# Two of six triangular inverses by halves of 16, joined on TensorE, and U's transpose from products of R and T

## The chip, the cores and the metric

The kernel runs on one core of one Trainium2 chip. The metric is the device time of one execution in microseconds (us), given as the median of several runs. The span in a profile, from the first to the last instruction, is some 2 us shorter. The **clock** is the granted clock of the matrix engine (TensorE, PE in the profile) as a share of full speed. In the records it is either 0.50 or 1.00, so a mean of 0.80 over a stretch says that 40% of the stretch ran at half clock.

## The reference, cut to what matters

```python
# r, k, v, w, a, b: (4 batches, 8 heads, 768 tokens, 40)
for t in range(S):
    y[:, :, t] = einsum('bhd,bhde->bhe', rt, state)
    Sa = einsum('bhde,bhe->bhd', state, at)
    state = state * wt[:, :, None, :] - einsum('bhd,bhe->bhde', Sa, bt)
    state = state + einsum('bhd,bhe->bhde', vt, kt)
# then, on all 3072 tokens (320 features, 2048 hidden)
h = x @ w_in
out = (h * clip(h + 3, 0, 6) / 6) @ w_out
```

## The kernel before

The scan over tokens is done in blocks of 64 tokens. Two batches make a unit of work, so there are 24 units ("steps"), and four units make a group. Within a block the effect of tokens on each other is a triangular system for each head. Its inverse T is worked out once for each group, for 32 heads and both batch halves together. There are six groups, so six inverses. The 64x64 inverse is put together from two inverses of 32x32 (substitution on VectorE, one row after another) and one off-diagonal block, which TensorE makes by two products (`third_block`).

```python
def invert(F, third):
    fb = inv.tile([P, L, L], F32, name="fb")
    nc.vector.transpose(out=..., in_=F[:, :, 0:L]...)
    x = inv.tile([P, L, L], F32, name="x", tag="x", bufs=1)
    # ... GpSimd masks fb into x, ones on the diagonal
    for i in range(1, L - 1):                  # 30 rows, two instructions each
        nc.vector.tensor_tensor(out=pv, in0=..., in1=..., op=ALU.mult)
        yield
        nc.vector.tensor_tensor(out=rest, in0=rest, in1=pv, op=ALU.add)
        yield
    # ... tb and tt: the inverse transposed, as TensorE wants it
def third_block(F, tb, tt, n):                 # products of F and tb, evicted as zs, then of tt and zs
    ...
```

A step takes T and makes U from it, then U's transpose, which feeds the scores:

```python
nc.tensor.matmul(out=up[x][half(x ^ s), pr, :], lhsT=tinv[...], rhs=R[...])   # U
...
x = turn_pairs(U)                              # four 128x128 transposes
UT = turned("UT"); nc.scalar.activation(out=UT[:], in_=x[:], func=AF.Copy)
x = scores(UT, RT, swap=True)
```

Each `yield` gives the builder of the program a place to put something else. In the first inverse this is the conversion of the feed-forward weights (`weights`), in the second it is feed-forward products (`pieces`). The program order of each engine is fixed at build time.

```python
while side:            # first group's inverse
    aside(1, 1)        # one step of the inverse, one step of conversion
...
for _ in range(16):    # second group's inverse
    aside(2)
    pieces(0.75)       # feed-forward products
...
# a feed-forward job may start only when:
i in ready and converted[0] >= (PIECES // 2 if i < SPLIT and r == 0 else PIECES)
```

A request for a feed-forward product is dropped when its job is not yet available. So the speed of the conversion decides how much feed-forward work lies early in the program.

Of the kernel before, what the change touches and what calls it, by code (L numbers as in the profile page):

```python
# [8 lines left out]
F32 = mybir.dt.float32  # L9
I32 = mybir.dt.int32  # L10
U32 = mybir.dt.uint32
ALU = mybir.AluOpType
# [4 lines left out]
P = 128  # L17
BL = 64
HB = BL // 2
L = 32  # L20
SLOT = 64


# [6 lines left out]
def kernel(  # L30
# [105 lines left out]
    def padded(t, name):  # L136
        nc.gpsimd.memset(t[:, :, D:SLOT], PADS.get(name, 0.0))
        return t
# [33 lines left out]

    values = [padded(const.tile([P, H, SLOT], F32, name=f"V{i}"), "V") for i in range(AHEAD)]
    inputs["R"] = padded(const.tile([P, H, SLOT], F32, name="R"), "R")

    tinv = const.tile([P, NH, BL], F32, name="tinv")

# [322 lines left out]
        yield DONE  # L500


    def invert(F, third):



        fb = inv.tile([P, L, L], F32, name="fb")
        nc.vector.transpose(out=fb[:].rearrange("p t s -> p s t"),
                            in_=F[:, :, 0:L].rearrange("p h s -> p s h"))
        x = inv.tile([P, L, L], F32, name="x", tag="x", bufs=1)  # L510
        nc.gpsimd.affine_select(out=x[:], in_=fb[:], pattern=[[1, L], [-1, L]],  # L511
                                compare_op=ALU.is_gt, fill=0.0, base=0, channel_multiplier=0)
        nc.gpsimd.memset(_ap(x[:], 0, [[L + 1, L]]), 1.0)
        for _ in range(3):
            yield
        for i in range(1, L - 1):
            n = L - 1 - i
            prod = inv.tile([P, L * L // 4], F32, name="prod")
            pv = prod[:, 0:n * i].rearrange("p (r j) -> p r j", j=i)
            nc.vector.tensor_tensor(  # L520
                out=pv, in0=_ap(x[:], (i + 1) * L + i, [[L, n], [0, i]]),
                in1=_ap(x[:], i * L, [[0, n], [1, i]]), op=ALU.mult,
            )
            yield
            rest = x[:, i + 1:L, 0:i]
            nc.vector.tensor_tensor(out=rest, in0=rest, in1=pv, op=ALU.add)  # L526
            yield
        tb = inv.tile([P, NH, L], F32, name="tb", tag="fb")
        nc.vector.transpose(out=tb[:].rearrange("p h t -> p t h"), in_=x[:])  # L529
        yield  # L530

        tt = inv.tile([P, NH, L], F32, name="tt")
        nc.vector.transpose(out=tt[:].rearrange("p h j -> p j h"),
                            in_=x[:].rearrange("p r j -> p j r"))
        third.append((F, tb, tt))
        for z in range(0, P, BL):
            yield
            nc.scalar.activation(out=tinv[z:z + L, :, 0:L], in_=tb[z:z + L], func=AF.Copy)
            nc.gpsimd.tensor_copy(tinv[z + L:z + BL, :, L:BL], tb[z + L:z + BL])
        yield  # L540

    def third_block(F, tb, tt, n):
        heads = slice(n * H, (n + 2) * H)
# [27 lines left out]
    def step(i):  # L571
# [21 lines left out]
                                     lhsT=o["at"][half(s, D), pr, half(q)],  # L593
                                     rhs=st[half(s, D), q, pr, 0:D], start=True, stop=True)
        yield PE
        R = tmp.tile([P, 2, NPR, D], F32, name="R")
        for s in range(2):
            nc.vector.tensor_tensor(out=R[:, s], in0=rp[s][:], in1=o["EV"][:, s], op=ALU.add)
        yield DONE
# [39 lines left out]
        yield DONE  # L639


        ysp = [ps_any([P, 2, 2, BL]) for _ in range(2)]
        for j in range(2):
            for q in range(2):
# [26 lines left out]
        for q in range(2):  # L671
            nc.vector.tensor_tensor(out=st[:, q, :, 0:D], in0=sn[q][:], in1=st[:, q, :, 0:D],  # L672
                                    op=ALU.add)
        yield DONE

        x = turn_pairs(U)
        yield PE
        UT = turned("UT")
        nc.scalar.activation(out=UT[:], in_=x[:], func=AF.Copy)
        yield DONE  # L680

        x = scores(UT, RT, swap=True)
# [177 lines left out]
    def by_twos(first, steps, mixed, rate, fill={}):  # L860


        chains = [prepared(first + i) for i in range(NU)]
        for t in range(TWOS):

            order = [0, 1] if t < STAGES else []
            order += [2, 3] if t > 5 else []
            if t == 3:
                order = [2, 3, 0, 1]
            for i in order:  # L870
                run(chains[i], steps if t > 10 else 0, fill.get(t, 0), mixed)
                pieces(rate / 2)
            if t == 10:
                side.append(invert(group_F[-1], third))
            yield


# [29 lines left out]
    for t in range(LAST + OWN):  # L907
        for i in range(NU):
            if 0 <= t - APART * i < OWN and t - APART * i != 11:
                if t - APART * i < 2:  # L910
                    block(i, t - APART * i)
                run(chains[i], weight=3)
        if t == LAST + 2:
            seconds()
            for name in "WA":
                fetch(name, NU + 1)
            third.clear()
            second_group = by_twos(NU, 3, 0, 1.25)
        if t in (LAST + 6, LAST + 8):

            name = "BK"[t > LAST + 6]
            others[name] = second(name)
            fetch(name, NU + 1)
        if t >= LAST + 6:
            next(second_group)
        elif t >= OWN + 1:
            pieces(1)
# [26 lines left out]
    def slot(i, rates, begin):  # L954
# [2 lines left out]
        before, own_chain[0] = own_chain[0], own  # L957
        for j, stages in enumerate((
                (before, own, ahead), (before, own, ahead, block, own), (block, own, ahead),
                (own, own, ahead), (own, pieces, ahead), (own, own, ahead), (own, ahead),  # L960
                (own, ahead))):
            if j == begin:
                side.append(invert(group_F[-1], third))
# [64 lines left out]
```

## Time and profile before

| | before |
|---|---|
| time, median of 3 runs | 882.01 us (881.49 to 888.24) |
| TensorE busy | 786.8 us, 89% of the span |
| VectorE busy | 536.8 us, 61% |
| mean granted clock | 0.94 |
| fifth state product (first of the second group) starts | 224.3 us |

### The profile page before, as it was taken

Reading aid. Unit: us, or ns where it says so; the run is one execution under the profiler, and the core shown is the slowest. Engines: PE = TensorE matmul, PEld = TensorE weight load, DVE = VectorE, ACT = ScalarE, POOL = GpSimd, SP = SyncE. Lnnn points to the kernel's source line nnn. Section 1 sums busy time; section 2 is a strip of 40 time slices with the busy share of each in tenths; the row PEclk is TensorE's granted clock in tenths of the full one; section 3 lists DMA queues with packets and bytes.
Section 4 is the critical chain, followed back from the end, with each engine's and each line's share of the span. In section 5 each row is a group of like instructions: output and inputs, shape, how many; then the busy total and the mean of one; then the engine's idle time right before and its main releaser. Section 6 shows DMA issues by size and latency. Waiting matters only on the chain.

```text
span 880.6 us, 34839 instructions
## 1 busy us (share of the span) xinstructions
PE 786.8 (89%) x15456; PEld 665.2 (76%) x15456; DVE 536.8 (61%) x1141; ACT 291.2 (33%) x670; POOL 148.8 (17%) x318
## 2 busy tenths in 40 slices
PE   4711977798799999999999999999999998999998
PEld 4511865686688888788888888888888887888886
DVE  7999678968854597643697454696455746222211
ACT  1334644232334322433323433233443223222211
POOL 4321011221121220321121122112012201000000
PEclk9755579998899999999999999999999999999999
DMA  6543344431223221222220222231232101000000
GB/s 132 93 103 102 103 112 97 75 64 24 39 41 64 54 46 30 56 38 47 55 56 17 52 48 48 41 57 33 41 57 45 25 15 26 18 20 19 18 17 16
DMA packets 175974, 45.00 MB, mean 51 GB/s; under 512 B 157904, under 2 KB 173264, under 8 KB 175824
## 3 DMA queue, kind: packets, MB, share of 16 engines
q1 hardware_dynamic: 174768, 42.61, 24.3%
q8 instruction: 122, 2.00, 0.9%
q10 hardware_dynamic: 1056, 0.16, 0.1%
q14 instruction: 28, 0.23, 0.1%
HBM read 34.08 MB, written 3.93 MB: 43 GB/s over the span
## 4 chain that ended last, share of the span: by engine, by line
PE 72%; DVE 5%; POOL 2%; issue 1%; ACT 0%; DMA 0%; SPq 0%; POOLq 0%; DVEq 0%; ACTq 0%
PE o L787 21%; PE h L763 18%; PE any L337 7%; PE h L768 6%; PE any L355 3%; PE any L665 2%; PE any L694 2%; PE any L429 2%; PE any L549 1%; PE any L647 1%; PE any L626 1%; PE any L561 1%; PE any L592 1%; PE any L611 1%; PE any L492 1%
## 5 line engine op out<-in xcount | busy, mean ns | idle before, releaser
L787 PE MATMUL o<-wout,gt 128*128 128x320 f32 x768 | 231.2, 442 | 0.5 <-DVE gt L774 0.5
L763 PE MATMUL h<-xt,win 128*128 128x128 f32 x1536 | 194.6, 278 | 0.0
L763 PEld LDWEIGHTS h<-xt,win 128*128 128x128 f32 x1536 | 184.2, 193 | 6.1
L787 PEld LDWEIGHTS o<-wout,gt 128*128 128x128 f32 x768 | 138.4, 191 | 50.5 <-issue 1.0
L774 DVE SCALAR_TENSOR_TENSOR gt<-gt,h 128x512 f32<-128x512 f32 x96 | 61.5, 682 | 83.1 <-ACT gt L773 82.9
L773 ACT ACTIVATE gt<-h,three 128x512 f32<-128x512 f32 x96 | 60.7, 683 | 116.1 <-PE h L768 116.0
L364 DVE COPY_PREDICATED score<-mask,any 128x256 f32<-128x256 int32 x143 | 54.9, 438 | 68.0 <-PE any L355 67.7
L520 DVE TENSOR_TENSOR prod<-x 128x30 f32<-128x30 f32 (+9 forms) x180 | 66.2, 368 | 10.0 <-POOL x L511 6.5
L526 DVE TENSOR_TENSOR x<-x,prod 128x30 f32<-128x30 f32 (+9 forms) x180 | 63.0, 350 | 4.8
L704 POOL TENSOR_TENSOR yg<-ys,gam 128x512 f32<-128x512 f32 x24 | 31.1, 1295 | 186.9 <-DVE ys L701 147.5
L768 PE MATMUL h<-xt,win 64*128 64x128 f32 x768 | 56.7, 288 | 0.0
L768 PEld LDWEIGHTS h<-xt,win 64*128 64x128 f32 x768 | 47.4, 190 | 6.1 <-issue 2.2
L549 PE MATMUL any<-tb,F 32*32 32x32 f32 x768 | 17.5, 203 | 34.8 <-DVE tb L529 34.0
L578 ACT ACTIVATE RT<-any 128x512 f32<-128x512 f32 x24 | 14.3, 596 | 91.5 <-PE any L337 91.5
L451 POOL MEMSET Kt<- 128x24 f32 x24 | 2.8, 118 | 238.0 <-PE any L694 238.0
L549 PEld LDWEIGHTS any<-tb,F 32*32 32x32 f32 x768 | 15.8, 118 | 36.0 <-issue 35.2
L379 DVE TENSOR_TENSOR_SCAN prods<-wm,start 128x528 f32<-128x528 f32 x24 | 30.4, 1267 | 19.2 <-ACT wm L376 17.4
L672 DVE TENSOR_TENSOR state<-any,state 128x160 f32<-128x160 f32 x48 | 13.1, 315 | 47.0 <-PE any L665 47.0
L404 DVE RECIPROCAL rgam<-prods 128x256 f32<-128x256 f32 x24 | 41.5, 1729 | 0.0
L390 DVE RECIPROCAL gam<-prods 128x256 f32<-128x256 f32 x24 | 41.3, 1734 | 0.0
L498 ACT ACTIVATE EV<-any 64x160 f32<-64x160 f32 x92 | 24.8, 294 | 43.6 <-PE any L492 43.1
L246 ACT ACTIVATE parts<-parts,low 128x256 uint32<-128x256 uint32 x40 | 20.3, 508 | 55.6 <-DVE parts L244 55.4
(138 smaller groups left out, 1193.6 us busy)
## 6 DMA issues: line engine op xcount, KB each, us to landing
raw<-in_moe_w_out_dram SPq DMA_DIRECT2D x20, 256.0 KB
B<-in_b_dram SPq DMA_DIRECT2D x48, 80.0 KB
K<-in_k_dram SPq DMA_DIRECT2D x48, 80.0 KB
V<-in_v_dram SPq DMA_DIRECT2D x96, 40.0 KB
R<-in_r_dram SPq DMA_DIRECT2D x96, 40.0 KB
out_dram<-ob SPq DMA_DIRECT2D x48, 80.0 KB
W<-in_w_dram SPq DMA_DIRECT2D x40, 80.0 KB
A<-in_a_dram SPq DMA_DIRECT2D x40, 80.0 KB
```

The source lines that it names most:

```text
L337: nc.tensor.transpose(out=o[:, n, :], in_=x[:, 2 * n:2 * n + 2, :].rearrange("p s e -> p (s e)"), identity=ident[:])
L364: nc.vector.copy_predicated(out=x[:, 4 * i:4 * i + 4, :], mask=mask4, data=o[i][:])
L390: nc.vector.reciprocal(gv[:, :, 0:HB], prods[:, :, 0, 1:HB + 1][:, :, ::-1])
L404: nc.vector.reciprocal(rv[:, :, HB:BL], prods[:, :, 1, 1:HB + 1])
L520: nc.vector.tensor_tensor(out=pv, in0=_ap(x[:], (i + 1) * L + i, [[L, n], [0, i]]), in1=_ap(x[:], i * L, [[0, n], [1, i]]), op=ALU.mult,)
L526: nc.vector.tensor_tensor(out=rest, in0=rest, in1=pv, op=ALU.add)
L549: nc.tensor.matmul(out=zp[x][z:z + L, h, :], lhsT=F[z + L:z + BL, n * H + h, L:BL], rhs=tb[z + L:z + BL, n * H + h, :], start=True, stop=True,
L763: nc.tensor.matmul(out=hp[c][:, i, :], lhsT=win[:, t, j * P:(j + 1) * P], rhs=xt[:, t, :], start=(t == 0 and i == 0), stop=False)
L768: nc.tensor.matmul(out=hp[c][:, i, :], lhsT=win2[half(c), (j0 + i) * P:(j0 + i + 1) * P], rhs=xt[half(c), 2, :], start=False, stop=(i == N ...
L773: nc.scalar.activation(out=gt[:], in_=hp[c][:], func=AF.Relu, bias=three[:], scale=1.0)
L774: nc.vector.scalar_tensor_tensor(out=gt[:], in0=gt[:], scalar=6.0, in1=hp[c][:], op0=ALU.min, op1=ALU.mult)
L787: nc.tensor.matmul(out=op[:], lhsT=gts[c][:, n, :], rhs=wout[:, c * HJ + r * NQ + n, :], start=((split or r == 0) and c == 0 and n == 0), ...
```

## The change

The intent: the first two inverses hold up TensorE, so they are made shorter on VectorE by solving two blocks of 16 at once (28 instructions in place of 60), and TensorE joins the halves. UT no longer waits for U: it comes straight from R and T. Left out of the cut below: R gets one fixed tile of its own (`RR`), and one fetch for the second group comes a step later.

```diff
-    def invert(F, third):
+    def invert(F, third, by_halves=False):
...
+        size, count = (L2, 2) if by_halves else (L, 1)
+        blocks = [size * (L + 1), count]
-        for i in range(1, L - 1):
+        for i in range(1, size - 1):
...
+        if by_halves:
+            yield from join_halves(F, tb, tt)
+    def join_halves(F, tb, tt):
+        for h in range(NH):                    # z: 128 products of 16 columns
+            for i in range(P // L):
+                nc.tensor.matmul(out=zp[i][z:z + L2, h, :], lhsT=F[z:z + L, h, 0:L2],
+                                 rhs=tb[z:z + L, h, L2:L], ...)
+        # six yields, zh = z (ScalarE), six yields
+        for h in range(NH):                    # x: 128 products of 16 columns
+            for i in range(P // L):
+                nc.tensor.matmul(out=xp[i][z:z + L2, h, :], lhsT=tt[z:z + L2, h, 0:L2],
+                                 rhs=zh[z:z + L2, h, L2:L], ...)
+        # tinv = x (ScalarE); lower part: 2 products on the identity, 64 products; four yields; tt
...
+        up = [ps_any([P, 2, P]) for _ in range(2)]      # U's transpose: 32 products
+        nc.tensor.matmul(out=up[x][half(rs), j, half(x ^ s)],
+                         lhsT=RR[half(x), s, pr * D:pr * D + SLOT],
+                         rhs=tinv[half(x), n * H + 4 * s + pr, :], ...)
-        x = turn_pairs(U)
-        UT = turned("UT")
...
-                side.append(invert(group_F[-1], third))
+                side.append(invert(group_F[-1], third, by_halves=True))   # groups 1 and 2 only
...
-                (own, own, ahead), (own, pieces, ahead), (own, own, ahead), (own, ahead),
+                (own, own, ahead), (own, own, pieces, ahead), (own, own, ahead), (ahead,),
```

More of the change, by code (lines that the diff above doesn't have):

```diff
@@ L20 @@
 L = 32
+L2 = L // 2
 SLOT = 64
@@ L174 @@
     inputs["R"] = padded(const.tile([P, H, SLOT], F32, name="R"), "R")
+    RR = const.tile([P, 2, NPR * D + SLOT - D], F32, name="RR")
+    nc.gpsimd.memset(RR[:, :, NPR * D:], 0.0)
     tinv = const.tile([P, NH, BL], F32, name="tinv")
@@ L513, in invert @@
         nc.gpsimd.memset(_ap(x[:], 0, [[L + 1, L]]), 1.0)
+        if by_halves:
+            nc.gpsimd.memset(x[:, L2:L, 0:L2], 0.0)
         for _ in range(3):
             yield
-        for i in range(1, L - 1):
-            n = L - 1 - i
+        size, count = (L2, 2) if by_halves else (L, 1)
+        blocks = [size * (L + 1), count]
+        for i in range(1, size - 1):
+            n = size - 1 - i
             prod = inv.tile([P, L * L // 4], F32, name="prod")
-            pv = prod[:, 0:n * i].rearrange("p (r j) -> p r j", j=i)
+            pv = _ap(prod[:], 0, [[n * i, count], [i, n], [1, i]])
             nc.vector.tensor_tensor(
-                out=pv, in0=_ap(x[:], (i + 1) * L + i, [[L, n], [0, i]]),
-                in1=_ap(x[:], i * L, [[0, n], [1, i]]), op=ALU.mult,
+                out=pv, in0=_ap(x[:], (i + 1) * L + i, [blocks, [L, n], [0, i]]),
+                in1=_ap(x[:], i * L, [blocks, [0, n], [1, i]]), op=ALU.mult,
             )
             yield
-            rest = x[:, i + 1:L, 0:i]
+            rest = _ap(x[:], (i + 1) * L, [blocks, [L, n], [1, i]])
             nc.vector.tensor_tensor(out=rest, in0=rest, in1=pv, op=ALU.add)
@@ L534, in invert @@
                             in_=x[:].rearrange("p r j -> p j r"))
-        third.append((F, tb, tt))
+        third.append((F, tinv[:, :, L:BL] if by_halves else tb, tt))
         for z in range(0, P, BL):
-            yield
+            if not by_halves:
+                yield
             nc.scalar.activation(out=tinv[z:z + L, :, 0:L], in_=tb[z:z + L], func=AF.Copy)
             nc.gpsimd.tensor_copy(tinv[z + L:z + BL, :, L:BL], tb[z + L:z + BL])
+        if by_halves:
+            yield from join_halves(F, tb, tt)
@@ L540, in invert @@
         yield
+    def join_halves(F, tb, tt):
+        zh = inv.tile([P, NH, L], F32, name="zh", tag="x", bufs=1)
+        nc.gpsimd.memset(zh[:, :, 0:L2], 0.0)
+        zp = [ps_any([P, NH, L2]) for _ in range(P // L)]
+        for h in range(NH):
+            for i in range(P // L):
+                z = i * L
+                nc.tensor.matmul(out=zp[i][z:z + L2, h, :], lhsT=F[z:z + L, h, 0:L2],
+                                 rhs=tb[z:z + L, h, L2:L], start=True, stop=True,
+                                 tile_position=(z, z))
+        for _ in range(6):
+            yield
+        for i in range(P // L):
+            z = i * L
+            nc.scalar.activation(out=zh[z:z + L2, :, L2:L], in_=zp[i][z:z + L2], func=AF.Copy)
+        for _ in range(6):
+            yield
+        xp = [ps_any([P, NH, L2]) for _ in range(P // L)]
+        for h in range(NH):
+            for i in range(P // L):
+                z = i * L
+                nc.tensor.matmul(out=xp[i][z:z + L2, h, :], lhsT=tt[z:z + L2, h, 0:L2],
+                                 rhs=zh[z:z + L2, h, L2:L], start=True, stop=True,
+                                 tile_position=(z, z))
+        yield
+        for i in range(P // L):
+            z = i * L
+            x = i % 2 * L + L2
+            nc.scalar.activation(out=tinv[z:z + L2, :, x:x + L2], in_=xp[i][z:z + L2],
+                                 func=AF.Copy)
+        lp = [ps_any([P, NH, L2]) for _ in range(2)]
+        for i in range(2):
+            z = i * BL
+            nc.tensor.matmul(out=lp[i][z:z + L], lhsT=ident[z:z + L, z:z + L],
+                             rhs=tt[z:z + L, :, 0:L2], start=True, stop=False,
+                             tile_position=(z, z))
+        for h in range(NH):
+            for i in range(2):
+                z = i * BL
+                nc.tensor.matmul(out=lp[i][z:z + L, h, :], lhsT=zh[z:z + L2, h, :],
+                                 rhs=tt[z:z + L2, h, 0:L2], start=False, stop=(h == NH - 1),
+                                 tile_position=(z, z))
+        for _ in range(4):
+            yield
+        for i in range(2):
+            z = i * BL
+            nc.scalar.activation(out=tt[z:z + L, :, 0:L2], in_=lp[i][z:z + L], func=AF.Copy)
@@ L595, in step @@
         yield PE
-        R = tmp.tile([P, 2, NPR, D], F32, name="R")
+        R = RR[:, :, 0:NPR * D].rearrange("p s (r d) -> p s r d", d=D)
         for s in range(2):
@@ L639, in step @@
         yield DONE
+        up = [ps_any([P, 2, P]) for _ in range(2)]
+        for j in range(2):
+            for s in range(2):
+                for x in range(2):
+                    for rs in range(2):
+                        pr = 2 * j + rs
+                        nc.tensor.matmul(out=up[x][half(rs), j, half(x ^ s)],
+                                         lhsT=RR[half(x), s, pr * D:pr * D + SLOT],
+                                         rhs=tinv[half(x), n * H + 4 * s + pr, :],
+                                         start=True, stop=True)
+        yield PE
+        UT = turned("UT")
+        for x in range(2):
+            nc.scalar.activation(out=UT[:, 2 * x:2 * x + 2], in_=up[x][:], func=AF.Copy, scale=-1.0)
+        yield DONE
         ysp = [ps_any([P, 2, 2, BL]) for _ in range(2)]
@@ L673, in step @@
                                     op=ALU.add)
-        yield DONE
-        x = turn_pairs(U)
-        yield PE
-        UT = turned("UT")
-        nc.scalar.activation(out=UT[:], in_=x[:], func=AF.Copy)
         yield DONE
@@ L918 @@
             second_group = by_twos(NU, 3, 0, 1.25)
-        if t in (LAST + 6, LAST + 8):
-            name = "BK"[t > LAST + 6]
+        if t in (LAST + 7, LAST + 8):
+            name = "BK"[t > LAST + 7]
             others[name] = second(name)
```

## The prediction

> **What bounds the kernel now.** I read the windows view first, cut at the events that the change touches (columns: busy time of each engine with its number of instructions, granted clock, DMA share, GB/s).

> ```profile
> 44.50:55.50 11.00, 2.73 (x64) 2.49 (x64) 10.61 (x35) 3.15 (x9) 5.34 (x9) 0.50 0.53 128
> 55.50:81.70 26.20, 0.00 (x0) 0.00 (x0) 26.20 (x92) 9.71 (x26) 0.00 (x0) 0.50 0.31 90
> 81.70:126.00 44.30, 35.60 (x851) 31.54 (x852) 33.21 (x101) 26.38 (x58) 5.79 (x12) 0.54 0.37 99
> 126.00:154.50 28.50, 22.31 (x555) 17.67 (x554) 22.72 (x65) 13.95 (x36) 4.79 (x8) 1.00 0.45 114
> 154.50:193.60 39.10, 33.98 (x739) 29.58 (x732) 31.26 (x39) 10.70 (x30) 8.45 (x22) 1.00 0.42 71
> 193.60:234.50 40.90, 30.95 (x385) 26.25 (x383) 36.14 (x77) 11.04 (x24) 8.44 (x19) 0.84 0.20 35
> 234.50:868.00 633.50, 626.76 (x12327) 529.75 (x12327) 339.23 (x679) 202.37 (x452) 99.76 (x201) 1.00 0.20 38
> ```

> From 234.5 us on TensorE is busy 626.8 of 633.5 us: there only TensorE work counts, and whatever the front leaves undone is paid in full at the end. From 55.5 to 81.7 TensorE does nothing and VectorE is never idle: this is the first group's inverse, alternating with the conversion of the weights. The second inverse lies in 193.6 to 234.5, where TensorE is idle 10 us. The timeline shows what ends these waits (start, duration, in brackets the idle time before and its releaser):

> ```profile
> 79.70 1.90 DVE L529 STREAM_TRANSPOSE tb<-x 128x1024 f32<-128x1024 f32 x1
> ...
> 81.74 1.92 PE L549 MATMUL any<-tb,F 32*32 32x32 f32 x64 [26.26 <-DVE tb L529]
> ...
> 87.74 1.92 PE L561 MATMUL any<-zs,tt 32*32 32x32 f32 x64
> ...
> 122.74 1.13 PE L355 MATMUL any<-RT,UT 40*64 40x64 f32 x32 [2.65 <-ACT UT L679]
> ...
> 229.88 1.92 PE L549 MATMUL any<-tb,F 32*32 32x32 f32 x64 [4.95 <-DVE tb L529]
> ```

> The two groups of instructions that the change cuts, from the page's table of groups (busy us, mean ns, idle before):

> ```profile
> L520 DVE TENSOR_TENSOR prod<-x 128x30 f32<-128x30 f32 (+9 forms) x180 | 66.2, 368 | 10.0 <-POOL x L511 6.5
> L526 DVE TENSOR_TENSOR x<-x,prod 128x30 f32<-128x30 f32 (+9 forms) x180 | 63.0, 350 | 4.8
> ```

> 180 of each are 30 for each of six inverses, so one inverse costs (66.2 + 63.0)/6 = 21.5 us of VectorE.

> [...] clock 0.50 from 44.5 to 81.7. [...] the timeline has TensorE back to back from 86.6 to 111.9 us on small products, still at 0.50, and full clock holds only from about 126, when the first 128x128 feed-forward products come. So I don't count on the join's tiny products to warm the clock. [...] 64 instructions of 40x32 tiles (L429 at 22.00 us, full clock) end after 0.85 us; less the last one's own 0.22 us that is 9.8 ns each. [...] the 128x30 update at 44.95 us took 0.87 us under a GpSimd product and 0.18 us at 79.27 us without.

> **The change, part by part.**

> *Substitution.* Two blocks of 16 in one instruction: 28 instructions in place of 60, of 28 to 112 elements. In the late part of the first inverse, five such instructions of 58 to 108 elements and five conversion steps took 78.63 - 76.42 = 2.21 us, 0.44 us a pair. 28 pairs are 12.4 us. Add four masked copies (1.5 us) and some 1.5 us of blocking by GpSimd at the beginning: from 44.6 to about 59.5 us, then the 1.9 us transpose, so TensorE starts at 61.5 rather than 81.7.

> *Join.* 128 products of 16 columns for z, 128 for x, 2 identity products of 512 columns and 64 of 32 columns; each is two instructions here (768 for the 384 feed-forward contractions). At about 11 ns (above, with four row positions), z and x take 256 x 11 = 2.8 us each. The last 128 instructions have two positions like L549, whose 64 take (1.92 - 0.2)/63 = 27 ns each at half clock: 3.4 us; identity some 1.7 us at half clock. Evictions are 586 ns each (the row of L555, 32x512): four for z and four for x, 2.4 us each, two for the lower part. One after the other: z to 64.5, eviction to 67.0, x to 70.0, then lower part to 75.1, third-block products to 76.9, their eviction to 78.2, with two or three ScalarE conversion steps between. L561 starts at 78.3 in place of 87.74: **-9.4 us**. The inverse gains 20 us, of which the join eats 11.

> *U's transpose.* Four 128x128 transposes (0.44 us back to back) give way to 32 instructions of 64x64 tiles, for which 64 take 1.09 us in L694, so 0.55 us. Over some 20 steps at the bound, 20 x 0.07 (taking half of the difference as hidden by pipelining) is **+1.4 us**. Two evictions of about 0.38 replace one of 0.6; ScalarE is not the bound. TensorE waited 4.7 us in all for UT, nearly all before 145 us (0.92, 2.65 and 1.12). UT is now ready two stages earlier. But the longest of these stood behind a ScalarE conversion step which waited for a weight transfer, so I count half: **-2.5 us**.

> *What moves: conversion and feed-forward.* The first inverse carried one conversion step with each of its own. With some 17 steps fewer it leaves conversion behind: by the order of instructions 14 pieces stood before the first state scaling, now 10. Four pieces at about 1.85 us (five VectorE steps) go into the second group's preparation. All 40 must be converted before the second feed-forward job may start, and requests made before that are lost. Counting in program order before the fifth step's first state product: before 92, 40 and 32 products of the three feed-forward lines, after 64, 32 and 22. At 0.112, 0.068 and 0.27 us an instruction (L763 x16 in 1.79, L768 x16 in 1.09, L787 x8 in 2.16), two each, the difference is 6.3 + 1.1 + 5.4 = **12.7 us** of TensorE work, which stays nearly 12 to 14 us at every later step. It is paid after 234.5, where TensorE has no slack. Taking it out of 154.5 to 193.6 gives little back: VectorE is busy 31.3 of 39.1 there, loses two pairs of feed-forward evictions and a sum (about 1.8 us net) and gains 5.6 us of conversion. I set that stretch unchanged.

> *Second inverse.* Without conversion between, dependent instructions of about 100 elements come every 0.29 us (203 to 205 us). 28 are 7.6; with blocking, masked copies and feed-forward evictions and GpSimd's mask before them, tb is ready some 20 us after the begin of its first transpose instead of 36. From there TensorE is bound: z 2.8, 16 feed-forward products 3.6, x 2.8, lower part 2.8 at full clock, then 9.2 of feed-forward, step products and transposes before L561's counterpart: 41.6 us in all against 234.48 - 193.63 = 40.9. **+0.7 us**: the idle time goes, and join work of the same size takes its place.

> Sum: 882.0 - 9.4 - 2.5 + 0.7 + 12.7 + 1.4 = 884.9.

> **Rivals.** *The join is issue-bound at half clock.* If its 16-column products take 27 ns as L549 does, z and x take 7 us each, the first group gains only 1 us and the time is about 893. For it: all 64-column products of 81.7 to 112 have 27 ns. Against: four row positions and narrow weights, and 9.8 ns seen at full clock. *The deferred feed-forward work is not lost.* If the preparation stretch shrinks by half of what leaves TensorE, because TensorE is continuous from 171.5 to 201 there, the time is about 878. *The clock returns earlier.* The new order puts U's products, scores and UT's products, all full-array tiles, one after another; before, such a stretch at 108 to 112 did release the clock for 4 us. Full clock from 100 on would save part of the 26 us of half-clock products, perhaps 6 us, VectorE allowing: about 878. *A whole 20 us gain arrives* (the join hidden, nothing deferred): 862; speaks against it that no other TensorE work stands in program order beside the first join, and that the lag of feed-forward work is in the order itself.

> **Range and chances.** The second and third rival are each likelier than the first, so I put the point under the sum: 880. Each main term has an error of 4 to 6 us, together about 10: range 867 to 893. 2% is 17.6 us. To be faster by that, the deferred work would have to be free as well; to be slower, both joins would have to cost double. Chances 0.11, 0.84 and 0.05.

> **What would show it.** In the changed kernel: the first tb transpose at about 59 us; L561's counterpart at 76 to 80 us; clock still 0.50 in the join; z and x products near 11 ns apart; the second group's preparation as long as before with less feed-forward work in it; TensorE continuous from the second join on; and at the end a longer unbroken run of feed-forward work, by 12 us, than before after the last step. Wrong if the first join lasts over 25 us, if conversion waits for transfers more than before, or if the preparation stretch shrinks by 8 us or more.

## More of the kernel before

From the page of the kernel before: busy time of TensorE and its number of products, the granted clock in 40 equal slices of the span (tenths), and one of the transfer queues (packets, MB, share):

```profile
PE 786.8 (89%) x15456; PEld 665.2 (76%) x15456; DVE 536.8 (61%) x1141; ACT 291.2 (33%) x670; POOL 148.8 (17%) x318
...
PEclk9755579998899999999999999999999999999999
...
q8 instruction: 122, 2.00, 0.9%
```

TensorE is almost always busy after the first quarter. The clock is half from slice 3 to 5.

## The result, and the profile after

The changed kernel took **917.19 us** (median of 4 runs, 915.26 to 919.73). Before took 881.75 us beside it (4 runs). The ratio is 1.0389, with a 95% interval of 1.0331 to 1.0446. So it is slower by 3.9%, where 880 was predicted with a range up to 893.

The parts of the page that answer those above:

```profile
PE 825.5 (90%) x17416; PEld 698.0 (76%) x17416; DVE 516.0 (56%) x1077; ACT 302.7 (33%) x714; POOL 149.5 (16%) x323
...
PEclk8755668597899999999999999999999998999999
...
q8 instruction: 137, 2.24, 1.0%
```

TensorE has 1,960 more products and is busy 39 us longer. There are 15 more packets in the instruction queue.

VectorE's saving is real. Groups of instructions of the stretch of the first two inverses (30 to 300 us), first before, then after (busy us, mean ns):

```profile
L526 DVE TENSOR_TENSOR x<-x,prod 128x30 f32<-128x30 f32 (+14 forms) x60 | 21.5, 358 | 1.0
L520 DVE TENSOR_TENSOR prod<-x 128x30 f32<-128x30 f32 (+14 forms) x60 | 21.4, 357 | 3.5 <-POOL x L511 2.6
```

```profile
L535 DVE TENSOR_TENSOR x<-x,prod 128x28 f32<-128x28 f32 (+6 forms) x28 | 9.0, 323 | 0.5
L529 DVE TENSOR_TENSOR prod<-x 128x28 f32<-128x28 f32 (+6 forms) x28 | 7.9, 283 | 1.8 <-POOL x L516 1.4
```

42.9 us of substitution have become 16.9 us. The windows of the changed kernel, cut at the same events as the prediction's windows (62.4 is the first join product, 85.2 the counterpart of L561, 196.2 the begin of the second inverse, 248.4 its L561 counterpart):

```profile
44.50:62.40 17.90, 2.76 (x65) 2.56 (x65) 17.90 (x62) 7.07 (x20) 4.24 (x10) 0.54 0.52 133
62.40:85.20 22.80, 13.53 (x712) 11.14 (x712) 10.07 (x27) 11.96 (x22) 4.00 (x8) 0.50 0.23 58
85.20:126.00 40.80, 34.70 (x873) 30.46 (x872) 26.16 (x84) 22.36 (x54) 2.75 (x5) 0.58 0.38 103
126.00:154.50 28.50, 23.54 (x521) 18.62 (x522) 23.85 (x70) 13.63 (x35) 3.97 (x7) 0.85 0.45 122
154.50:196.20 41.70, 32.08 (x706) 26.57 (x705) 35.14 (x55) 13.74 (x40) 9.09 (x23) 0.75 0.40 73
196.20:248.40 52.20, 42.80 (x1016) 35.88 (x1015) 23.76 (x47) 15.48 (x30) 9.34 (x21) 0.80 0.13 25
248.40:900.00 651.60, 639.53 (x12951) 542.91 (x12951) 340.41 (x681) 204.14 (x474) 98.70 (x201) 0.99 0.19 38
```

Two things stand out. In the first join (second line) TensorE is busy only 13.5 of 22.8 us, though VectorE is busy less than half of that time. The stretch of the second inverse (sixth line) takes 52.2 us where it took 40.9. The waits of TensorE around the first inverse and join say what the idle time is (line, releaser, us in total, times, longest). Before, 55 to 90 us:

```profile
PE any L549 <- DVE tb L529: 26.3, 1, 26.3
```

After, 62.0 to 85.3 us:

```profile
PE any L563 <- DVE parts L253: 7.4, 1, 7.4
PE any L563 <- issue: 4.9, 2, 2.8
PE any L577 <- issue: 3.5, 2, 2.6
PE any L577 <- ACT zh L570: 0.9, 2, 0.5
```

The wait of 26.3 us is down to 7.4 us, as intended. (The view names L253, which ended last, at 62.38 us; the transpose of tb ended at 62.25.) But 8.4 us are new, in four gaps whose releaser is "issue". That is time in which the engine waited for nothing that the profile shows, so for no semaphore of another engine.

The second join in the timeline of the changed kernel (start, duration, idle before it and its releaser):

```profile
217.37 2.16 PE L563 MATMUL any<-tb,F 32*16 32x16 f32 x175 [1.92 <-DVE tb L538]
221.11 0.86 PE L563 MATMUL any<-tb,F 32*16 32x16 f32 x81 [1.58 <-issue]
221.91 6.21 PE L836 MATMUL h<-xt,win 128*128 128x128 f32 x32
228.04 1.34 PE L577 MATMUL any<-zh,tt 16*16 16x16 f32 x143
230.13 1.06 PE L577 MATMUL any<-zh,tt 16*16 16x16 f32 x111 [0.75 <-issue]
...
233.86 3.28 PE L595 MATMUL any<-tt,zh 16*32 16x16 f32 x117 [0.73 <-issue]
```

The gaps are here too, 3.1 us in all. The 32 feed-forward products between z and x take 6.2 us. The same 32 at full clock took 3.73 us in the kernel before, at 210.12 us of its timeline.

**Where the time went.** I followed the start of each step's state product through both traces. The table gives its shift against the kernel before (us). The last column is what is added after the 24th product.

| stretch | shift of after against before | added in this stretch |
|---|---|---|
| up to the 4th product (first inverse) | -0.8 | -0.8 |
| 4th to 6th (second preparation and inverse) | +11.4 | +12.2 |
| 6th to 24th product | +22.2 | +10.8 |
| after the 24th product (feed-forward tail) | +34.4 | +12.2 |

So four things have to be explained: a gain of 9 us that didn't come, 12 us at the second inverse, a slow creep of 11 us, and a tail of 12 us. Only the tail was in the prediction.

### The profile page after: what moved, and what is told of

Same layout as the page of the kernel before. It is cut to its first block, busy times and chain, and to the rows that moved or that the text cites. A ratio compares the mean times of both kernels' runs of the same rounds, so it can differ in the third digit from the quotient of the medians.

```text
span 915.0 us, 38729 instructions
## 1 busy us (share of the span) xinstructions
PE 825.5 (90%) x17416; PEld 698.0 (76%) x17416; DVE 516.0 (56%) x1077; ACT 302.7 (33%) x714; POOL 149.5 (16%) x323
## 4 chain that ended last, share of the span: by engine, by line
PE 72%; DVE 4%; issue 2%; POOL 1%; ACT 1%; DMA 0%; SPq 0%; DVEq 0%
PE o L860 20%; PE h L836 19%; PE any L341 5%; PE h L841 5%; PE any L359 3%; PE any L767 2%; PE any L744 2%; PE any L433 2%; PE any L611 1%; PE any L710 1%; PE any L688 1%; PE any L623 1%; PE any L654 1%; PE any L673 1%; DVE tb L538 1%
## 5 line engine op out<-in xcount | busy, mean ns | idle before, releaser
L860 PE MATMUL o<-wout,gt 128*128 128x320 f32 x768 | 234.3, 447 | 0.2 <-DVE gt L847 0.2
L836 PE MATMUL h<-xt,win 128*128 128x128 f32 x1536 | 200.2, 285 | 0.5 <-DVE gt L847 0.5
L836 PEld LDWEIGHTS h<-xt,win 128*128 128x128 f32 x1536 | 189.9, 199 | 6.5 <-DVE gt L847 0.7
L860 PEld LDWEIGHTS o<-wout,gt 128*128 128x128 f32 x768 | 140.3, 194 | 51.9 <-issue 3.0
L847 DVE SCALAR_TENSOR_TENSOR gt<-gt,h 128x512 f32<-128x512 f32 x96 | 61.7, 685 | 134.6 <-ACT gt L846 134.5
L535 DVE TENSOR_TENSOR x<-x,prod 128x84 f32<-128x84 f32 (+14 forms) x148 | 55.3, 374 | 3.1
L529 DVE TENSOR_TENSOR prod<-x 128x84 f32<-128x84 f32 (+14 forms) x148 | 48.5, 328 | 9.3 <-POOL x L516 5.3
L383 DVE TENSOR_TENSOR_SCAN prods<-wm,start 128x528 f32<-128x528 f32 x24 | 30.5, 1271 | 17.5 <-ACT wm L380 16.6
L774 DVE TENSOR_TENSOR ys<-any,ys 128x256 f32<-128x256 f32 x48 | 18.1, 418 | 30.2 <-PE any L767 30.2
L878 ACT ACTIVATE ob<-o 128x320 f32<-128x320 f32 x23 | 10.1, 437 | 64.7 <-issue 37.8
```

Source lines behind the costliest of these rows:

```text
L529: nc.vector.tensor_tensor(out=pv, in0=_ap(x[:], (i + 1) * L + i, [blocks, [L, n], [0, i]]), in1=_ap(x[:], i * L, [blocks, [0, n], [1, i]]) ...
L836: nc.tensor.matmul(out=hp[c][:, i, :], lhsT=win[:, t, j * P:(j + 1) * P], rhs=xt[:, t, :], start=(t == 0 and i == 0), stop=False)
L847: nc.vector.scalar_tensor_tensor(out=gt[:], in0=gt[:], scalar=6.0, in1=hp[c][:], op0=ALU.min, op1=ALU.mult)
L860: nc.tensor.matmul(out=op[:], lhsT=gts[c][:, n, :], rhs=wout[:, c * HJ + r * NQ + n, :], start=((split or r == 0) and c == 0 and n == 0), ...
```

## The experiments

The outputs are right. The steps are compared with those of the kernel before in the same way as above.

### Taking the change apart

`inverse_only` has both inverses by halves, but U's transpose, its places in the schedule and the transfers as before:

```diff
-        up = [ps_any([P, 2, P]) for _ in range(2)]      # the 32 products for UT
+        x = turn_pairs(U)                                # four transposes, at the old place
```

> The inverse by halves in both groups, U transposed as before. Theory A (the inverse does nearly all the harm: join held by gaps in the supply of instructions, feed-forward work deferred, clock lost): 25 to 34 us over the kernel before, and the profile keeps a creep of some 8 us between the sixth and the last step. Rival B (U's products, 28 more instructions a step, cause the 10.8 us that the changed kernel loses between the sixth and the last step): 20 to 24 us over before, without that creep.

`ut_only` keeps the old inverses and has the new UT:

```diff
-                side.append(invert(group_F[-1], third, by_halves=True))
+                side.append(invert(group_F[-1], third))
```

> U's transpose by products, both inverses in the old way. Theory A: within 4 us of before, possibly 1 to 3 us faster because the early waits for UT go. Rival B: 8 to 11 us slower than before, lost evenly over the steps.

`first_only` and `second_only` have the new UT, and halves in one of the two groups:

```diff
+        t0 = first                             # the group's first unit
-                side.append(invert(group_F[-1], third, by_halves=True))
+                side.append(invert(group_F[-1], third, by_halves=(t0 == 0)))   # first_only
+                side.append(invert(group_F[-1], third, by_halves=(t0 > 0)))    # second_only
```

> As the changed kernel, but only the first group's inverse by halves. Theory A: the deferred feed-forward work (12.7 us) is all from the first group, since only there does the conversion of weights ride on the inverse; with the loss of clock in the second group's preparation 12 to 18 us over before. Rival C (the joins are the loss and both cost the same): about half of the changed kernel's 35 us, and so no difference between this one and the next.

> As the changed kernel, but only the second group's inverse by halves. Theory A: no feed-forward work is deferred; the join stands in the way of TensorE for some 20 us where the old inverse left it idle for 10: 8 to 15 us over before. Rival C: 17 us, the same as the first group alone.

Measured (3 rounds; before 883.84 us, 7 runs; the shifts are of one profiled execution each):

| kernel | median, us | ratio (95%) | 4th product | 4th to 6th | 6th to 24th | tail |
|---|---|---|---|---|---|---|
| inverse_only | 908.70 | 1.0257 (1.0197 to 1.0317) | -1.0 | +13.9 | +1.9 | +12.3 |
| ut_only | 885.79 | 1.0007 (0.9958 to 1.0056) | +1.8 | +1.8 | +2.8 | -0.3 |
| first_only | 908.33 | 1.0262 (1.0208 to 1.0315) | -0.3 | +4.6 | +8.3 | +12.2 |
| second_only | 898.34 | 1.0130 (1.0072 to 1.0188) | -0.7 | +13.6 | +2.5 | -0.3 |

What follows: the UT products alone cost nothing that can be told from zero. The tail of 12.2 us comes with halves in the *first* group, whatever else is there. Of the 12 to 14 us between the 4th and 6th product, most come with halves in the *second* group; without them it is 1.8 or 4.6. The first group by halves gains at most 1 us by the fourth product, which is no more than single profiles differ there: `second_only`, with the old first inverse, has -0.7, and `ut_only` +1.8. The creep is large only where halves in the first group and the new UT come together.

### Is it the number of instructions?

In the trace of the changed kernel the first join's products come in runs of 125 to 128 between the gaps, at some 10 ns a product (128 in 1.24 us). The transfer records show packets of 16,384 bytes on the instruction queue, six of them in the join. The page has 17,416 pairs of a load and a product for 137 packets, and 15,456 for 122 before: 127 pairs a packet in both. So by my estimate from these counts a packet brings the instructions of about 128 pairs. The four gaps of the first join end 2.3 to 2.5 us after the begin of such a packet.

```diff
+    dummy = ps_any([P, NH, 16])
+    for h in range(320):                      # ready long before, never read
+        z = h % 4 * L
+        nc.tensor.matmul(out=dummy[z:z + 16, h // 4 % NH, :], lhsT=ident[z:z + L, 0:16],
+                         rhs=ident[z:z + L, 16:32], ...)
     while side:
         aside(1, 1)
```

> The kernel before, with 320 products of 32x16 on the identity (640 pairs of load and product, nothing to wait for, never read) put where TensorE idles during the first inverse. Theory (instruction supply): bursts of about 128 pairs at some 10 ns a pair with standing gaps of 2 to 3 us between them that no semaphore explains, in all 16 to 19 us. Rival (the gaps in the join come from its own waits): one unbroken run of about 6.5 us. The kernel's time should hardly move, as TensorE idles there for 26 us.

Measured: one run, 884.18 us. Its timeline on TensorE, from the first of these products to the first of the kernel's own:

```profile
55.72 1.24 PE L890 MATMUL any<-ident 32*16 32x16 f32 x126
58.34 1.26 PE L890 MATMUL any<-ident 32*16 32x16 f32 x128 [1.38 <-issue]
62.34 1.26 PE L890 MATMUL any<-ident 32*16 32x16 f32 x128 [2.74 <-issue]
66.62 1.26 PE L890 MATMUL any<-ident 32*16 32x16 f32 x128 [3.02 <-issue]
70.35 1.26 PE L890 MATMUL any<-ident 32*16 32x16 f32 x128 [2.46 <-issue]
73.81 0.23 PE L890 MATMUL any<-ident 32*16 32x16 f32 x2 [2.19 <-issue]
82.06 1.92 PE L549 MATMUL any<-tb,F 32*32 32x32 f32 x64 [8.03 <-DVE tb L529]
```

This is the mechanism by itself. The 640 pairs took 18.3 us, in runs of exactly 128 with gaps of 1.4 to 3.0 us and not one semaphore. The transfer records of the same trace have five instruction packets, starting at 55.76, 59.72, 64.15, 67.72 and 71.46 us. The next run of products starts 2.58, 2.62, 2.47, 2.63 and 2.35 us after each. Four runs of 128 take (73.81 - 58.34)/4 = 3.87 us each, which is **30 ns a pair**, against 9.8 ns within a run. The rival's 6.5 us is excluded.

Do other transfers hold the packets up? They took 0.32 of the transfer engines' time in these 18.3 us and 0.05 in the second join of the changed kernel (217.3 to 237.1 us), and there too the gaps end 2.4 to 2.6 us after the begin of a packet. So the delay from a packet was no longer at 0.32 than at 0.05. And "issue" alone is not the sign: the wait of 2.4 us that the kernel before has in its second preparation ends 5.3 us after the last such packet, and what it is stays open.

`join_bf16` then takes instructions out of the join. The z and x products work on the upper halves of their words, so each is one pair and not two (with both mendings the stretch from the second inverse to the fifth state product has 667 products in the trace, against 920 in `catch_up`), with everything else the same. It is less exact on purpose.

```diff
-                nc.tensor.matmul(out=zp[i][...], lhsT=F[z:z + L, h, 0:L2],
-                                 rhs=tb[z:z + L, h, L2:L], ...)
+                nc.tensor.matmul(out=zp[i][...], lhsT=F[z:z + L, h, 0:L2].bitcast(BF16)[:, 1::2],
+                                 rhs=tb[z:z + L, h, L2:L].bitcast(BF16)[:, 1::2], ...)
```

> The changed kernel with the 128 z and 128 x products of each join on the upper halves of their words, so that each is one load and one product in place of two: 256 pairs fewer in each join, everything else the same; the result is allowed to be less exact, on purpose. Theory (the join is limited by the supply of instructions, some 128 pairs per 3.7 us): the number of standing gaps in a join falls by two, so each join is 4 to 8 us shorter and the time 8 to 14 us below the changed kernel's, 903 to 909. Rival (the gaps come from something else than the number of instructions, for instance the waits for the banks or the half clock): same gaps, under 4 us gained.

Measured (3 rounds): 902.46 us (898.86 to 907.35), ratio 1.0219 (1.0167 to 1.0270). That is 14.7 us below the changed kernel's median, a little over the range that I had given. The waits in its first join, 62 to 80 us:

```profile
PE any L564 <- DVE tb L539: 7.3, 1, 7.3
PE h L578 <- DVE win L269: 3.7, 1, 3.7
PE any L578 <- ACT zh L571: 1.3, 3, 0.4
```

There is no "issue" gap left. What now shows is a wait of 3.7 us ahead of x, while ScalarE copies to tinv, converts and then evicts z (the first eviction starts at 67.00 us, x at 67.62). The prediction had 2.4 us for this eviction. L561's counterpart starts at 78.89 us, where 78.3 was predicted, and the first state product at 80.7 us, 8.9 us earlier than before. That is the -9.4 us of the prediction, which appear once the join has half as many z and x pairs. The shifts by stretches are -9.1, +6.9, +12.3 and +12.2 us.

### Is the deferred feed-forward work lost?

`catch_up` is the changed kernel with the conversion hurried in the first join, so that the feed-forward products stand in program order exactly as before the change. The trace confirms it: 184, 80 and 64 instructions of the three feed-forward lines lie ahead of the fifth state product, as before, and 128, 64 and 44 in the changed kernel.

```diff
+    count = 0
     while side:
-        aside(1, 1)
+        count += 1
+        aside(1, 1 + (count > 9))
```

> The changed kernel with the first join's remaining conversion steps taken two at a time, so that the feed-forward products stand in program order exactly as before the change (43.3 us of them ahead of the fifth state product in place of 30.5, by my count from the trace's durations). Theory (the 12.7 us of deferred feed-forward work is paid at the end, and the same deferral lets the array's clock fall in the second preparation and makes the 10.8 us creep of steps 5 to 23): the tail after the last step is 12 us shorter, the creep falls to 2 to 4 us, and up to 7 us are given back because four pieces of conversion again lie beside the first inverse; time 896 to 907. Rival (the deferral alone costs the 12 us, the creep belongs to the UT products): 905 with the creep still over 8 us. Second rival (deferral harmless): 917.

Measured (3 rounds): 896.26 us (894.96 to 897.71), ratio 1.0140 (1.0102 to 1.0177). The tail is back (-0.3 us in place of +12.2), and so is most of the creep (+1.7 us in place of +10.8). The other terms stay: +0.4 at the fourth product, +13.5 from there to the sixth; of the up to 7 us that I thought would be given back, 1.2 were. One small change of program order gave back 20.9 us (ratio 1.0389 to 1.0140, in different rounds). So the deferral cost more than the work deferred: once in the tail, and again as creep. The clock alone doesn't explain the creep. From 250 us to the end the changed kernel runs 19.1 us at half clock, before 3.7, `catch_up` 8.6, which would fit. But `ut_only` has 12.5 us and a creep of 2.8, and `first_only` 6.8 us and a creep of 8.3.

### Can long products between the short ones hide the gaps?

In `spread` the second join is issued in lots of 16 products with feed-forward work in between. The first join and the total of feed-forward work are unchanged.

```diff
+            if spread and h % 4 == 3:          # after each 16 join products
+                yield
-    for _ in range(16):
+    for _ in range(28):
         aside(2)
-        pieces(0.75)
+        pieces(12 / 28)
```

> The changed kernel with the second join's products in lots of 16 and the same 12 shares of feed-forward work of that stretch put between the lots; the first join and everything else in program order unchanged. Theory (the second join costs 11 us by starved instruction supply and by the half clock that the long run of tiny products brings): with long products between the lots the fetches stay ahead and the clock stays up, so the fifth step after it starts 4 to 9 us earlier and the time is 908 to 913. Rival (the join's cost is the dependent evictions or the lost VectorE overlap): no gain, 917.

Measured (3 rounds): 923.49 us (920.49 to 928.30), ratio 1.0458 (1.0409 to 1.0507). This is **slower** than the changed kernel, and both the gain that I expected and the rival's 917 are wrong. That a long run of tiny products brings the half clock, and long ones between keep it up, was my assumption: the clock of the stretch was 0.74 here and 0.79 in the changed kernel. The stretch from the begin of the second inverse to the fifth state product, first in the changed kernel, then in `spread`:

```profile
196.20:244.10 47.90, 38.50 (x903) 32.11 (x902) 20.18 (x43) 13.71 (x27) 8.20 (x16) 0.79 0.10 20
```

```profile
196.50:249.90 53.40, 42.16 (x907) 33.28 (x905) 20.31 (x43) 13.94 (x27) 8.41 (x17) 0.74 0.10 18
```

The same work takes 5.5 us more: 3.7 of busy time at a lower clock (0.74 in place of 0.79), and 1.8 of idle time. The join's gaps fell from 3.1 to 2.3 us. But the spread shares of feed-forward work were now missing ahead of the join, where TensorE stood 4.6 us and not 1.9. My edit had moved two things. `spread_front` keeps the work ahead of the join and lays only the 16 products between z and x between lots:

```diff
-        pieces(12 / 28)
+        pieces(0.75 if n < 8 else 0.3)
```

> The run spread lost 6 us though only one supply gap was left in its join: it had moved feed-forward work from before the join to behind it (idle before the join 4.6 us in place of 1.9), and its clock was lower (0.74 in place of 0.79 over the join's stretch). Here all the feed-forward work ahead of the join stays as in the changed kernel, and only the 16 products between z and x are laid between lots of 64 to 128 pairs. Theory as mended (idle before the join plus clock explain spread): the join's gaps fall from 3 us to under 1.5, and what comes out is decided by the clock: 912 to 917 if it stays at 0.79, up to 921 if long and short products in turn lower it to 0.74 again. Rival (the lots themselves are slow, for instance through the change of tile shapes): 921 or more with the clock at 0.79 and no more idle time.

Measured (3 rounds): 918.70 us (917.50 to 920.36), ratio 1.0392 (1.0352 to 1.0432), the same as the changed kernel. The gaps fell to 1.75 us (0.31 and 1.44; I had said under 1.5), and the stretch took 48.7 us at a clock of 0.72:

```profile
198.70:247.40 48.70, 40.63 (x903) 32.99 (x901) 20.29 (x43) 13.99 (x28) 8.42 (x17) 0.72 0.12 21
```

So 1.3 us of gaps won were paid back by 2.1 us more of busy time, at a lower clock (0.72 in place of 0.79). Spreading does not help here. TensorE was busy 40.6 of 48.7 us here and 38.5 of 47.9 in the changed kernel, so the busy share alone did not tell the clock. Why it was lower in the two runs that alternate long and short products (0.74 and 0.72) is not shown by these runs.

### What is left with both mendings?

`first_exact_catch_up` has halves in the first group only, the old UT, and the conversion caught up. `first_bf16_catch_up` is the same with the z and x products on upper halves. `bf16_catch_up` is the whole change with both mendings.

```diff
-                side.append(invert(group_F[-1], third, by_halves=True))
+                side.append(invert(group_F[-1], third, by_halves=(first == 0)))   # the two first_ kernels
```

> The inverse by halves in the first group only, U transposed as before the change, and the conversion caught up so that the feed-forward products keep their old order. Theory (in the first group the starved instruction supply eats what the shorter substitution gains; the rest of the loss was deferral and the second join, both absent here): within 4 us of the kernel before, 880 to 886. Rival (the halves themselves harm the later steps): over 890. Rival of the prediction's arithmetic (the first join is worth 9 us): 873 to 876.

> The same with the z and x products of the first join on the upper halves of their words, half as many pairs, less exact on purpose. Theory: no standing gap in the join, the first state product 7 to 9 us earlier than in the exact version, and nearly all of it kept to the end, as no work is deferred: 872 to 878, the first version below the kernel before. Rival (an early start is lost again before the fourth step, because VectorE's conversion or the transfers of the weights bound that stretch): 880 to 884.

> The whole change with both mendings: bf16 halves in both joins and the conversion caught up. Theory (the two costs are independent): 917.2 less 20.9 (catch_up) less 14.7 (join_bf16) gives 882, range 878 to 886, that is the time of before; what is left against first_bf16_catch_up, some 5 to 8 us, is the second join's own work and half clock where TensorE is already the bound, and the UT products. Rival (the two mendings gained the same microseconds): 890 or more.

Measured beside 882.52 us of before (11 runs):

| kernel | median, us (range, runs) | ratio (95%) | 4th product | 4th to 6th | 6th to 24th | tail |
|---|---|---|---|---|---|---|
| first_exact_catch_up | 889.23 (882.03 to 890.80, 6) | 1.0042 (1.0003 to 1.0080) | +1.5 | +3.3 | +2.3 | 0.0 |
| first_bf16_catch_up | 879.81 (878.80 to 886.63, 6) | 0.9976 (0.9945 to 1.0008) | -4.8 | +1.5 | +0.3 | 0.0 |
| bf16_catch_up | 882.61 (881.09 to 884.06, 4) | 0.9993 (0.9964 to 1.0021) | -5.2 | +3.8 | +0.6 | -0.3 |

The sum for `bf16_catch_up` was 917.2 - 20.9 - 14.7 = 882, and it came out at 882.6. So the two costs are separate, and together they are nearly the whole loss. Its second join shows no supply gap in the waits from 189 to 240 us. The "issue" wait of 1.7 us lies before products of the preparation, not in the join:

```profile
PE any L497 <- issue: 1.7, 1, 1.7
PE any L497 <- DVE score L369: 1.6, 1, 1.6
```

The stretch from the 4th to the 6th product costs 3.8 us with half as many z and x pairs, and 13.5 us with all of them (`catch_up`).

The two first-group kernels were both a little slower than I had expected. The exact one has runs at 882 to 883 us and at 889 to 891 us. Its profile fell in the longer kind, so its steps in the table are of a long run. The kernel before has both kinds too (881.72 to 883.84 and 887.91 to 889.25 us in the seven runs of the first round), and so the profile of `ut_only`, a run of 888.48 us, may be of the longer one. What parts the two kinds is not settled. The bf16 one starts 5.6 us earlier at the first state product, not the 7 to 9 I expected, and keeps about 3 of them. It is the only version below the kernel before, by 0.24%, with an interval that reaches over 1, and it is less exact. No version that beats the kernel before is established.

## Why the prediction was wrong

**The intent and the VectorE side were right.** The first tb transpose was predicted at about 59 us (the terms given add up to 60.0) and started at 60.34. Substitution fell from 42.9 to 16.9 us. The clock stayed at 0.50 in the first join, as predicted.

**The step that failed first: "At about 11 ns (above, with four row positions), z and x take 256 x 11 = 2.8 us each."** The duration is right: a run of 128 pairs takes 1.24 to 1.26 us, 9.8 ns a pair. What failed is the use of it for 256 pairs in a row. It came from a run of 64 pairs, half a packet by the estimate above, that no gap interrupted (0.85 us). The kernel before has the other kind too: at 39.75 us a run of 64 stops after its first product for 1.20 us of "issue", and goes on 2.75 us after the begin of a packet. Over longer bursts the supply limited: `ready_products` has 30 ns a pair over 640, with a gap after each 126 or 128. By the prediction's clockwork TensorE was to start at 61.5 and finish x at 70.0. It started at 62.4 and finished x at 77.4. The rest came as worked out: the lower part took 5.1 us (5.1 predicted), the third-block products 1.9 us. So L561's counterpart started at 85.21 and not at 78.3, and the term of -9.4 us was -2.5 us, of which -0.8 us were left at the fourth state product. `join_bf16` shows that the 9 us are there when the number of pairs is halved. The sign that I had named, a first join of over 25 us, did not fire: it lasted 22.8 us, where my clockwork has 16.8.

The first rival, "the join is issue-bound at half clock", had the right size (27 ns a pair) for a wrong reason. Runs in the first join, at a clock of 0.50, go at 9.8 ns. I argued against it with exactly that number, and so threw the right size away with the wrong reason. The two rivals for which I put the point under the sum did not come: the deferred work was not free, and the clock did not return earlier (0.58 from 85.2 to 126 us, and 0.85 from there to 154.5, where it had been 1.00). The trace of the kernel before has full clock from 112.3 to 115.7 us, after products with no wait from 106.3 to 111.9; that those released it was my reading.

**"+0.7 us: the idle time goes, and join work of the same size takes its place."** This was +11.3 us (52.2 against 40.9), and +13.5 us to the sixth product with the feed-forward order kept (`catch_up`). The front part was right: tb was to be ready 20 us after the begin, and the join's first product started 21.2 us after it. From there the prediction had 21.6 us (its terms add up to 21.2) and the trace has 31.0. The idle time did not go: 9.4 us are left of 9.95, because the gaps (3.1 us), the wait for tb (1.9) and an "issue" wait of 4.4 us ahead of the join, which ends 7.8 us after the last packet and so is not of the same kind, took the place of the waits before. Most of the remainder goes with the clock. I had assumed full clock, and the stretch had 0.80, at half from 220.1 to 226.9 and from 233.7 to 240.6 us. The 16 feed-forward products (32 instructions) took 6.2 us and not 3.6, identity and lower part 5.4 us (231.0 to 237.1, less a gap of 0.7) and not 2.8, and what follows 11.3 and not 9.2. How far this clock is itself a result of the gaps was not separated. The fall from 13.5 to 3.8 us in `bf16_catch_up` holds the gaps, the pairs saved and what they bring along.

**The 12.7 us of deferred feed-forward work were right**, by their mechanism and size: +12.2 or +12.3 us in the tail of every kernel that has the deferral, and none where it is absent. What was wrong is what surrounds them. **"I set that stretch unchanged"**: the preparation stretch from 154.5 us took 41.7 us and not 39.1, at a clock of 0.75 and not 1.00. The clock goes with the deferral: 0.75 to 0.88 from 154.5 us to the second inverse in the six kernels that have it, 0.95 to 1.00 in the others. The cut at 154.5 us hides what the length does. From the fourth product to the begin of the second inverse it is 57.0 us before, 56.8 to 59.3 in the others without deferral, and 60.0 to 61.7 in the six with it; 4.4 of the 4.6 us that `first_only` adds from the 4th to the 6th product lie here. And the deferral brought the creep, which the prediction doesn't have at all. The added time from the 6th to the 24th product sorts the kernels cleanly:

| | feed-forward order as before | deferred |
|---|---|---|
| U transposed | +2.3, +0.3 | +1.9 |
| UT products | +2.8, +2.5, +1.7, +0.6 | +10.8, +8.3, +12.3, +9.7, +9.8 |

(First row: first_exact_catch_up, first_bf16_catch_up; inverse_only. Second row: ut_only, second_only, catch_up, bf16_catch_up; after, first_only, join_bf16, spread, spread_front.) In these kernels it comes only where both are present (for deferral with U transposed there is one kernel). Why is not shown, but the windows say what the creep is made of. From the 6th to the 24th product, before, after and `first_only`:

```profile
260.66:814.52 553.86, 547.12 (x11158) 463.28 (x11157) 314.85 (x635) 183.11 (x413) 93.16 (x189) 1.00 0.21 40
272.07:836.72 564.65, 552.58 (x11657) 468.95 (x11656) 316.25 (x638) 184.80 (x433) 92.09 (x189) 0.98 0.21 40
264.96:827.07 562.11, 548.79 (x11657) 465.83 (x11656) 316.54 (x638) 185.15 (x433) 92.31 (x189) 0.99 0.22 40
```

TensorE's idle time rises from 6.7 us to 12.1 and 13.3. Of the busy time, 1.4 us are deferred feed-forward work that comes back here, by the prediction's durations. What is left for the lower clock is about 4 us in the changed kernel and next to nothing in `first_only`. So idle time is about half of the creep in the one and most of it in the other. With UT products and no deferral (`ut_only`, `catch_up`) it is 9.1 us, with deferral and U transposed (`inverse_only`) 5.0. Some of it is the supply of instructions again: the changed kernel has 3.4 us of "issue" gaps here, before 0.7, and each ends 2.2 to 2.5 us after the begin of a packet. But `ut_only` has 3.3 as well, so they don't explain why the deferral matters.

**"+1.4 us" for the UT products was right within what can be measured:** over the 6th to 24th product they took 9.3 us, where the transposes took 8.9, and `ut_only` is at a ratio of 1.0007. (By the figures of the prediction, half of 0.11 us over 20 steps, the term would be 1.1.) The **-2.5 us** of UT waits did not show. `ut_only` is 1.8 us later at the fourth product, not earlier.

The account by stretches, the prediction's terms put where they belong (us, span of the profiled runs):

| stretch | predicted | measured |
|---|---|---|
| up to the 4th product | -9.4 - 2.5 = -11.9 | -0.8 |
| 4th to 6th | +0.7 | +12.2 |
| 6th to 24th | +1.4 | +10.8 |
| tail | +12.7 | +12.2 |
| sum | +2.9 | +34.4 |

## What to carry to other kernels

Count the instructions of a burst, not only their durations. Here a rate taken from a short run did not hold for a long one: products of 32x16 took 9.8 ns a pair within a run of 128, and 30 ns a pair over the 640 of `ready_products`. The sign of it was a gap released by "issue" after each 126 or 128 pairs, which ended 2.35 to 2.63 us after the begin of a packet of the instruction queue. When a change shortens one engine's work, check in the program order what was waiting for a place beside that work: here it was the conversion of weights, whose delay took feed-forward products out of idle time and put them at the end. And if two mendings are each measured alone, measure them together too; only that showed that the two costs add up.
